# Cutting the last attention chunk into four one-tile blocks, and dropping the filler matmuls

## The chip, the cores and the metric

One core of a Trainium2 chip runs the whole program in one launch. The metric is the device time of that launch in microseconds (us). The kernel before has a median of 1463.39 us in four runs (1460.27 to 1465.49).

Engine names are those of the profile: PE is the matrix engine, PEld its weight loads, DVE the vector engine, ACT the scalar engine, POOL the GpSimd engine, SPq the queue that issues the DMAs.

A ratio in this text is the mean time of one kernel's fast runs over the mean time of the fast runs of the kernel before in the same rounds. It is therefore not quite the ratio of the medians that stand beside it.

## The reference

A layer norm feeds a 32-head attention and a SwiGLU, and both are added to the input. S = 2048, D = 512, head size 16.

```python
xn  = layernorm(A_x)                               # [1, 2048, 512]
q,k,v = split(xn @ wqkv)                           # 32 heads of 16
p   = softmax(q @ k.T * 16**-0.5)                  # 2048 x 2048 for each head
att = (p @ v) @ wo
glu = (silu(xn @ w1) * (xn @ w3)) @ w2
out = A_x + att + glu
```

## The kernel before

Attention is done in 32 blocks: 8 groups of 4 heads, times 4 chunks of 512 queries. A block goes through two stages, and the second stage of block n runs beside the first stage of block n+1.

1. Max: PE makes the scores with the queries on the partitions, DVE takes row maxima (32 reductions of 128x1024). The negated maxima go through POOL, a DVE transpose and nine DMAs, and become two extra rows of the query operand `QM`.
2. Exp: PE makes the scores again with the keys on the partitions. The extra rows of `QM` subtract the maximum. ACT takes `exp` (64 tiles of 128x512), PE multiplies by V ("PV"), ACT copies the result, three DMA steps bring the reciprocal row sums to where POOL multiplies with them.

```python
def max_block(n):
    g, cc = blocks[n]                              # 4 tiles of 128 queries in a chunk cc
    for tl_ in range(4):
        for kc in range(NCH):
            for j0 in (0, 1):
                u = max_units[mu_ctr[0] % 2]       # PSUM banks (0,1) or (2,3)
                ...                                # 2 matmuls into u, reduce_max of u     (L846, L857)
    ...                                            # negate, split in two, transpose       (L861..L873)
    S.dma(... scr_nm[par] <- NMT ...)              #                                       (L875)
    for j in range(4):
        for hl in range(2):
            S.dma(... QM[prt, r, j % 2, cc*512:(cc+1)*512] <- scr_nm ...)              # (L885)
```

Ahead of the exps stands a filler. It is a dummy matmul after every second exp from number 1900 on (there are 2048), meant to keep the clock of PE up, and it writes PSUM bank 3:

```python
FILL_BANK = 3
...
S.add("act", emit_ex, ...)                         # exp                                   (L923)
if fill_from is not None and idx >= fill_from and (idx - fill_from) % fill_every == 0:
    def emit_fill(e):
        return e.matmul(bank(FILL_BANK), IDENT, ...)                                   # (L930)
    fill_tasks.append(S.add("pe", emit_fill, ..., writes=[hz_bank[FILL_BANK]], extra=[ta], stream="fill"))
```

The output projection of a 128-row tile needs all 8 head groups. What it waits for is kept per chunk of 512 queries:

```python
S.add("pool", ... ATTNT[:, g, cc*512:(cc+1)*512] = OT * RB ..., writes=[hz_attnt[g][cc]])   # (L1002)
...
for t0 in range(0, NT, 2):
    cc = t0 // 4
    chains.append(dict(..., reads=[hz_attnt[g][cc] for g in range(G)] + [hz_wop]))          # (L684)
```

All instructions of an engine run in an order that is fixed when the program is built: a small scheduler inside the source plans it from estimated durations, and dependencies follow the order in which the source names the buffers. Whatever writes bank 3 earlier in the source must be done before a later writer of bank 3.

Of the kernel before, what the change touches and what calls it, by code (L numbers as in the profile page):

```python
# [359 lines left out]
def bass_parallel_sum__mha_block__glu_gated_swiglu__prompt_kernel(  # L360
# [15 lines left out]
    if A_x.shape[1] == 2048 and A_x.shape[2] == 512 and B_w1.shape[1] == 1792:  # L376
        cfg.setdefault("max_after", "glu2_0_0_0")
        cfg.setdefault("fill_from", 1900)
        cfg.setdefault("fill_every", 2)
    ACT_EXP_DUR = cfg.get("act_exp_dur", 500)  # L380
    FILL_BANK = 3
# [18 lines left out]
    PV_BATCH = 3  # L400
    NBLK = G * NCH
# [60 lines left out]
    with ExitStack() as stack:  # L462
# [87 lines left out]
        hz_qm = [[[_Buf("qm%d_%d_%d" % (r, v, cc)) for cc in range(NCH)] for v in range(2)] for r in range(R_QM)]  # L550
# [43 lines left out]
        S.add("pool", lambda e: e.memset(VAUG[:, :, :, 0:1], 1.0), writes=hz_vaug, dur=200 + NT * H, name="vones", stream="init")  # L594

# [151 lines left out]
        for r in range(R_QM):  # L747
            for v in range(2):
                for cc in range(NCH):
                    hz_qm[r][v][cc].inherit(*hz_xn)  # L750
# [57 lines left out]
        blocks = [(g, cc) for g in range(G) for cc in range(NCH)]  # L808
# [22 lines left out]
        def max_block(n):  # L831
            g, cc = blocks[n]
            r = g % R_QM
            par = n % 2
            for tl_ in range(4):
                qt = 4 * cc + tl_
                for kc in range(NCH):
                    for j0 in (0, 1):
# [3 lines left out]
                        def emit_mm(e, u=u, j0=j0, qt=qt, kc=kc, tl_=tl_):  # L842
                            ins = None
                            for i, j in enumerate((j0, j0 + 2)):
                                h = j // 2
                                ins = e.matmul(bank(u[i]), QM[64 * h:64 * h + 64, r, j % 2, qt * 128:(qt + 1) * 128],  # L846
                                               KAUG[64 * h:64 * h + 64, g, kc * 512:(kc + 1) * 512],
                                               start=True, stop=True, tile_position=(64 * h, 0))
                            return ins
                        S.add("pe", emit_mm, reads=[hz_qm[r][j0 % 2][cc], hz_kaug[g][kc]], writes=[hz_bank[u[0]], hz_bank[u[1]]],  # L850
                              extra=[max_gate[0]] if (n == 0 and tl_ == 0 and kc == 0 and j0 == 0) else [],
                              dur=216, name="maxS%d_%d_%d_%d" % (n, tl_, kc, j0), stream="max", mode="64x128")
                        base = tl_ * 4 * NCH + j0 * NCH + kc
                        st = 2 * NCH

                        def emit_mx(e, u=u, base=base, st=st, par=par):
                            return e.reduce_max(MPART[:, par, base:base + st + 1:st],  # L857
                                                ps[:, u[0] * 512:(u[0] + 2) * 512].rearrange("p (a b) -> p a b", a=2), axis=AX.X)
                        S.add("dve", emit_mx, reads=[hz_bank[u[0]], hz_bank[u[1]]], pwrites=[hz_mpart[par]], dur=1139,
                              name="max%d_%d_%d_%d" % (n, tl_, kc, j0), stream="max")  # L860
            S.add("dve", lambda e, par=par: e.tensor_reduce(MFIN[:, par, :], MPART[:, par, :].rearrange("p (a k) -> p a k", k=NCH),  # L861
                                                           AX.X, ALU.max),
                  reads=[hz_mpart[par]], writes=[hz_mfin[par]], dur=135, name="mfin%d" % n, stream="small")
            nmv = NM[:, par, :].rearrange("p (t l j) -> p t l j", t=4, l=2, j=4)
            S.add("pool", lambda e, par=par: e.tensor_scalar(T32[:, par, :], MFIN[:, par, :], -4.0, 0.0, op0=ALU.mult, op1=ALU.add),  # L865
                  reads=[hz_mfin[par]], writes=[hz_t32[par]], dur=250, name="t32_%d" % n, stream="negm")
            S.add("pool", lambda e, par=par, nmv=nmv: e.tensor_scalar(nmv[:, :, 0, :], T32[:, par, :].rearrange("p (t j) -> p t j", t=4),
                                                                    1.0, 0.0, op0=ALU.mult, op1=ALU.add),
                  reads=[hz_t32[par]], writes=[hz_nm[par]], dur=250, name="nmhi_%d" % n, stream="negm")
            S.add("pool", lambda e, par=par, nmv=nmv: e.tensor_tensor(nmv[:, :, 1, :], T32[:, par, :].rearrange("p (t j) -> p t j", t=4),  # L870
                                                                    nmv[:, :, 0, :], ALU.subtract),
                  reads=[hz_t32[par], hz_nm[par]], writes=[hz_nm[par]], dur=300, name="nmlo_%d" % n, stream="negm")
# [5 lines left out]
            for j in range(4):  # L878
                for hl in range(2):
                    prt = 32 * j + 16 + hl  # L880

                    def emit_sc(e, j=j, hl=hl, prt=prt, par=par):
                        dst = QM[prt:prt + 1, r, j % 2, cc * 512:(cc + 1) * 512]
                        src = scr_nm[par].rearrange("(b t k) x -> k t b x", b=4, t=4, k=8)[4 * hl + j]
                        return e.dma_start(dst, src)  # L885
                    S.dma(emit_sc, reads=[hz_scrnm[par]], pwrites=[hz_qm[r][j % 2][cc]], nbytes=1024, name="nmsc%d_%d_%d" % (n, j, hl),
                          stream="nmt", ring="nmt", group=grp)
# [14 lines left out]
        fill_tasks = []  # L902

        def emit_exp_unit(tiles):
# [5 lines left out]
            n, kt, j = tile  # L910
            g, cc = blocks[n]
            r = g % R_QM
            h = j // 2

            def emit_mm(e):
                return e.matmul(bank(b), KAUG[64 * h:64 * h + 64, g, kt * 128:(kt + 1) * 128],  # L916
                                QM[64 * h:64 * h + 64, r, j % 2, cc * 512:(cc + 1) * 512],
                                start=True, stop=True, tile_position=(64 * h, 0))
            S.add("pe", emit_mm, reads=[hz_kaug[g][kt // 4], hz_qm[r][j % 2][cc]], writes=[hz_bank[b]], dur=216,
                  name="expS_%d_%d_%d" % tile, stream="exp", mode="64x128")  # L920
# [7 lines left out]
            if fill_from is not None and idx >= fill_from and (idx - fill_from) % fill_every == 0:  # L928
                def emit_fill(e):
                    return e.matmul(bank(FILL_BANK), IDENT, KAUG[:, g, kt * 128:kt * 128 + 512] if kt * 128 + 512 <= S_ else KAUG[:, g, 0:512],  # L930
                                    start=True, stop=True)
                fill_tasks.append(S.add("pe", emit_fill, reads=[hz_const, hz_kaug[g][kt // 4]], writes=[hz_bank[FILL_BANK]], extra=[ta],
                                        dur=216, name="fill%d" % idx, stream="fill", mode="128x128"))
# [7 lines left out]
        pvstate = {}  # L941

        pv_pending = []

        def flush_pv():
# [5 lines left out]
            def emit_pv(e, sets=sets):  # L951
                ins = None
                for (n, kt, slots) in sets:
                    g, cc = blocks[n]
                    for j in range(4):
                        ins = e.matmul(ps[32 * j:32 * j + 17, PVB * 512:(PVB + 1) * 512], VAUG[:, kt, 4 * g + j, :],  # L956
                                       PT[:, slots[j], :], start=(kt == 0), stop=(kt == NKT - 1), tile_position=(0, 32 * j))
                return ins
            rd = []
            for (n, kt, slots) in sets:  # L960
                rd += [hz_pt[s_] for s_ in slots] + [hz_vaug[kt]]
            S.add("pe", emit_pv, reads=rd, writes=[hz_bank[PVB]], dur=232 * len(sets),
                  name="pv%d_%d_x%d" % (sets[0][0], sets[0][1], len(sets)), stream="pv", mode="128x32")

        def yield_pv():
            while True:
# [3 lines left out]
                keys = [(n, kt, j) for j in range(4)]  # L970
# [3 lines left out]
                pv_pending.append((n, kt, slots))  # L974
                for k in keys:
                    del tile_slot[k]
                last = (kt == NKT - 1)
                if len(pv_pending) >= PV_BATCH or last:
# [8 lines left out]
        def finish_block(n):  # L987
            g, cc = blocks[n]
            rr = n % 2
            S.add("act", lambda e, rr=rr: e.activation(OT[:, rr, :], bank(PVB), ACT.Copy), reads=[hz_bank[PVB]], writes=[hz_ot[rr]],  # L990
                  dur=690, name="pvev%d" % n, stream="pvevac")
            S.dma(lambda e, rr=rr: e.dma_start(LC[:, rr, :], OT[0:128:32, rr, :]), reads=[hz_ot[rr]], writes=[hz_lc[rr]],
                  nbytes=8192, name="lgath%d" % n, stream="norm", ring="norm")
            S.add("dve", lambda e, rr=rr: e.reciprocal(RC[:, rr, :], LC[:, rr, :]), reads=[hz_lc[rr]], writes=[hz_rc[rr]],  # L994
                  dur=250, name="recip%d" % n, stream="nrm")
            S.dma(lambda e, rr=rr: e.dma_start(scr[rr], RC[:, rr, :]), reads=[hz_rc[rr]], writes=[hz_scr[rr]],
                  nbytes=8192, name="rc2d%d" % n, stream="norm", ring="norm")
            grp = []
            for j in range(4):
                S.dma(lambda e, rr=rr, j=j: e.dma_start(RB[32 * j + 1:32 * j + 17, rr, :], scr[rr, j:j + 1, :].broadcast_to([16, 512])),  # L1000
                      reads=[hz_scr[rr]], pwrites=[hz_rb[rr]], nbytes=32768, name="rbb%d_%d" % (n, j), stream="norm", ring="norm", group=grp)
            S.add("pool", lambda e, rr=rr, g=g, cc=cc: e.tensor_tensor(ATTNT[:, g, cc * 512:(cc + 1) * 512], OT[:, rr, :], RB[:, rr, :], ALU.mult),  # L1002
                  reads=[hz_ot[rr], hz_rb[rr]], writes=[hz_attnt[g][cc]], dur=1270, name="attn%d" % n, stream="attn")

        LAG = 1
        for n in range(NBLK + LAG):
            if n < NBLK:
                g, cc = blocks[n]
                if cc == 0 and g + 1 < G:
                    pass  # L1010
                if cc == 0 and g >= 1:
# [3 lines left out]
            if m >= 0:  # L1015
                for kt in range(NKT):
                    for j in range(4):
                        pend.append((m, kt, j))
                    form_units()
        form_units(flush=True)  # L1020
        yield_pv()
# [89 lines left out]
```

## Time and profile before

| what | value | view |
|---|---|---|
| time | 1463.39 us (4 runs) | times |
| DVE busy from 300 to 1300 us | 98.8% | windows |
| block 30: exps on ACT | 1356.89 to 1390.77 us | timeline of ACT |
| block 31 (the last): max ends | 1390.91 us | timeline of DVE |
| ACT idle before block 31's exps | 8.61 us, and 0.71 us before the copy | timeline of ACT |
| last exp to the end of the span | 20.7 us | timeline, page |

These two lines are from the page of the kernel before: the engines' shares of the chain that ended last, and the costliest group (line, engine, operation, shapes, count, busy us, mean ns, idle before).

```profile
DVE 66%; PE 25%; ACT 4%; SPq 2%; DMA 2%; issue 1%; POOL 0%; POOLq 0%
L857 DVE TENSOR_REDUCE arena<-ps 128x2 f32<-128x1024 f32 x1024 | 1170.6, 1211 | 172.8 <-PE ps L846 167.8
```

The row maxima on DVE carry two thirds of the chain that ended last. They bound the long middle of the kernel, which the change leaves alone. The change is about what comes after them. The next lines are the timeline of ACT at the end: start, duration, line, operation, count, and in brackets the idle time before and what ended it.

```profile
1390.17 0.60 ACT L923 ACTIVATE arena<-ps 128x512 bf16<-128x512 f32 x1 [0.37 <-PE ps L916]
1391.48 0.60 ACT L990 ACTIVATE arena<-ps 128x512 f32<-128x512 f32 x1 [0.71 <-PE ps L956]
1400.68 1.57 ACT L923 ACTIVATE arena<-ps 128x512 bf16<-128x512 f32 x3 [8.61 <-PE ps L916]
...
1405.28 3.08 ACT L923 ACTIVATE arena<-ps 128x512 bf16<-128x512 f32 x6 [0.50 <-PE ps L916]
...
1435.36 2.07 ACT L923 ACTIVATE arena<-ps 128x512 bf16<-128x512 f32 x4 [0.27 <-PE ps L916]
1437.96 0.60 ACT L990 ACTIVATE arena<-ps 128x512 f32<-128x512 f32 x1 [0.53 <-PE ps L956]
```

ACT finishes block 30, copies, and then waits 8.61 us, because the maxima of block 31 end only at 1390.9 and their DMAs have to follow. From 1405.28 to 1437.43 it does 58 exps, 0.554 us each. Last, the timeline of PE from the last PV on, and two windows of the same stretch (after the interval and its length: PE, PEld, DVE, ACT and POOL busy, granted PE clock, DMA share, GB/s).

```profile
1437.84 9.67 PE L930 MATMUL ps<-arena 128*128 128x512 bf16 x43
1447.35 7.07 PE L684 MATMUL ps<-arena 128*128 128x512 bf16 x32
1454.26 3.62 PE L930 MATMUL ps<-arena 128*128 128x512 bf16 x16
1440.00:1444.00 4.00, 4.00 (x20) 1.86 (x19) 0.25 (x1) 0.00 (x0) 0.00 (x0) 1.00 0.11 19
1444.00:1448.00 4.00, 3.95 (x20) 1.76 (x18) 0.00 (x0) 0.00 (x0) 1.26 (x1) 1.00 0.05 16
```

During the normalisation by DMA (1438.6 to 1445.5) PE runs fillers (L930), the clock stays at 1.00, and the projection of the last four tiles (32 matmuls) takes 7.07 us.

### The profile page before, as it was taken

How to read it: one execution, taken by the hardware profiler on the slowest of the kernel's cores; microseconds unless marked ns; L12 is line 12 of the kernel's file. 1: busy time of each engine (PE TensorE's matmuls, PEld its weight loads, DVE VectorE, ACT ScalarE, POOL GpSimd, SP SyncE). 2: the span in 40 equal slices, each digit the busy share in tenths (PEclk: the TensorE clock that was granted, in tenths of full speed). 3: DMA queues.
4: the chain of work that ended last, by engine and by line, in shares of the span. 5: the costliest groups of instructions: out<-in, count | busy, mean ns of one | idle time of the engine just before them, and what ended most of it. 6: DMA issues, size and time to landing. Idle time of an engine off the chain costs nothing.

```text
span 1458.1 us, 20711 instructions
## 1 busy us (share of the span) xinstructions
PE 1294.4 (89%) x8144; PEld 391.1 (27%) x8170; DVE 1217.4 (83%) x1215; ACT 1182.5 (81%) x2299; POOL 182.2 (12%) x225
## 2 busy tenths in 40 slices
PE   3999999989888899888888888888998888888889
PEld 2334432322222222222222222222222222222223
DVE  7000089999999999999999999999999999998831
ACT  1775542379999999999899999999999998888764
POOL 0205543320010001000100010001000000000000
PEclk9999999999999999999999999999999999998999
DMA  6000000010000000000000000000000000000011
GB/s 252 2 2 0 1 1 1 1 16 5 6 5 6 6 5 8 6 6 5 6 5 6 5 6 5 5 6 5 6 5 6 5 6 5 6 5 5 5 34 34
DMA packets 31138, 18.39 MB, mean 13 GB/s; under 512 B 21056, under 2 KB 27456, under 8 KB 31040
## 3 DMA queue, kind: packets, MB, share of 16 engines
q1 hardware_dynamic: 31040, 17.06, 4.4%
q8 instruction: 64, 1.05, 0.3%
q14 instruction: 34, 0.28, 0.1%
HBM read 14.16 MB, written 2.62 MB: 12 GB/s over the span
## 4 chain that ended last, share of the span: by engine, by line
DVE 66%; PE 25%; ACT 4%; SPq 2%; DMA 2%; issue 1%; POOL 0%; POOLq 0%
DVE arena L857 64%; PE ps L684 13%; PE ps L704 4%; ACT arena L923 4%; PE ps L846 3%; PE ps L916 3%; SPq L885 2%; PE ps L956 1%; PE ps L930 1%; DMA arena<-scr_nm 1%; DVE arena L613 1%; DMA scr_nm<-arena 1%; DVE arena L629 0%; DVE arena L994 0%; DMA arena<-arena 0%
## 5 line engine op out<-in xcount | busy, mean ns | idle before, releaser
L857 DVE TENSOR_REDUCE arena<-ps 128x2 f32<-128x1024 f32 x1024 | 1170.6, 1211 | 172.8 <-PE ps L846 167.8
L923 ACT ACTIVATE arena<-ps 128x512 bf16<-128x512 f32 x2048 | 1029.3, 644 | 98.1 <-PE ps L916 93.3
L916 PE MATMUL ps<-arena 64*128 64x512 bf16 x2048 | 688.9, 391 | 71.7 <-DMA arena<-scr_nm 16.4
L846 PE MATMUL ps<-arena 64*128 64x512 bf16 x2048 | 438.7, 393 | 59.1 <-DVE arena L857 44.3
L916 PEld LDWEIGHTS ps<-arena 64*128 64x128 bf16 x2048 | 181.1, 94 | 490.7 <-ACT arena L923 440.6
L684 PE MATMUL ps<-arena 128*128 128x512 bf16 x841 | 202.7, 382 | 6.2 <-POOL arena L785 3.8
L846 PEld LDWEIGHTS ps<-arena 64*128 64x128 bf16 x2048 | 99.8, 93 | 318.0 <-DVE arena L857 266.9
L956 PE MATMUL ps<-arena 128*17 128x512 bf16 x2048 | 146.6, 385 | 1.0 <-ACT arena L923 0.9
L1002 POOL TENSOR_TENSOR arena<-arena 128x512 bf16<-128x512 f32 x32 | 40.5, 1266 | 623.7 <-DMA arena<-scr_rinv 623.7
L684 PEld LDWEIGHTS ps<-arena 128*128 128x128 bf16 x864 | 74.9, 98 | 109.5 <-issue 25.4
L785 POOL TENSOR_TENSOR arena<-arena 128x512 bf16<-128x512 bf16 x56 | 64.5, 1152 | 89.5 <-ACT arena L783 89.5
L704 PE MATMUL ps<-arena 128*16 128x512 bf16 x1024 | 61.4, 386 | 1.2 <-DVE arena L649 0.9
L956 PEld LDWEIGHTS ps<-arena 128*17 128x17 bf16 x2048 | 36.9, 89 | 72.3 <-issue 50.9
L801 ACT ACTIVATE arena<-ps 128x512 f32<-128x512 f32 x16 | 9.8, 610 | 56.1 <-PE ps L684 56.1
L783 ACT ACTIVATE arena<-ps 128x512 bf16<-128x512 f32 x56 | 33.4, 597 | 26.6 <-PE ps L684 26.6
L781 ACT ACTIVATE arena<-ps 128x512 bf16<-128x512 f32 x56 | 33.4, 597 | 25.5 <-PE ps L684 25.5
L865 POOL TENSOR_SCALAR arena<-arena 128x16 f32<-128x16 f32 x32 | 6.6, 206 | 373.4 <-DVE arena L861 373.0
L1047 DVE TENSOR_TENSOR arena<-ps,arena 128x512 bf16<-128x512 f32 x16 | 11.1, 691 | 46.7 <-PE ps L684 46.7
L739 POOL TENSOR_SCALAR arena<-arena 128x2048 bf16<-128x2048 bf16 x16 | 31.4, 1977 | 125.3 <-PE ps L916 65.2
L704 PEld LDWEIGHTS ps<-arena 128*16 128x16 bf16 x1024 | 20.4, 89 | 41.9 <-ACT arena L712 13.5
L712 ACT ACTIVATE arena<-ps,arena 128x512 bf16<-128x512 f32 x32 | 24.9, 778 | 8.1 <-PE ps L704 6.7
L643 PE MATMUL ps<-arena 128*128 128x128 bf16 x64 | 7.5, 312 | 24.2 <-DVE arena L629 24.2
(45 smaller groups left out, 178.9 us busy)
## 6 DMA issues: line engine op xcount, KB each, us to landing
arena<-in_B_w_dram SPq DMA_DIRECT2D x3, 1792.0 KB, 19.0
arena<-scr_nm SPq DMA_DIRECT2D x256, 1.0 KB
arena<-scr_rinv SPq DMA_DIRECT2D x128, 32.0 KB, 1.8
arena<-in_A_x_dram SPq DMA_DIRECT2D x4, 512.0 KB, 6.1
out_dram<-arena SPq DMA_DIRECT2D x16, 128.0 KB, 1.7
arena<-in_A_wqkv_dram SPq DMA_DIRECT2D x1, 1536.0 KB, 11.8
scr_nm<-arena SPq DMA_DIRECT2D x32, 8.0 KB, 1.4
arena<-in_A_wo_dram SPq DMA_DIRECT2D x4, 128.0 KB, 4.3
```

The source lines that it names most:

```text
L684: ins = e.matmul(ps[:, ch["bank"] * 512:ch["bank"] * 512 + ch["n"]], ch["lhs"](kk), ch["rhs"](kk), start=(kk == 0), stop=(kk == nk - 1))
L704: ins = e.matmul(ps[32 * j:32 * j + DH, b * 512:(b + 1) * 512], WQKV[:, dc, hcol:hcol + DH], XNT[:, dc, tc * 512:(tc + 1) * 512], start=(d ...
L739: S.add("pool", lambda e, r=r, v=v, msk=msk: e.tensor_scalar(QM[:, r, v, :], QUN[:, g, :], msk, 0.0, op0=ALU.mult, op1=ALU.add), reads=hz_ ...
L781: S.add("act", lambda e, bg=bg, rg=rg: e.activation(SG[:, rg, :], bank(bg), ACT.Silu), reads=[hz_bank[bg]], writes=[hz_sg[rg]], dur=600, n ...
L783: S.add("act", lambda e, bu=bu, rg=rg: e.activation(UB[:, rg, :], bank(bu), ACT.Copy), reads=[hz_bank[bu]], writes=[hz_ub[rg]], dur=690, n ...
L785: S.add("pool", lambda e, rg=rg, fc=fc: e.tensor_tensor(HT[:, fc, :], SG[:, rg, :], UB[:, rg, :], ALU.mult), reads=[hz_sg[rg], hz_ub[rg]], ...
L846: ins = e.matmul(bank(u[i]), QM[64 * h:64 * h + 64, r, j % 2, qt * 128:(qt + 1) * 128], KAUG[64 * h:64 * h + 64, g, kc * 512:(kc + 1) * 51 ...
L857: return e.reduce_max(MPART[:, par, base:base + st + 1:st], ps[:, u[0] * 512:(u[0] + 2) * 512].rearrange("p (a b) -> p a b", a=2), axis=AX.X)
L916: return e.matmul(bank(b), KAUG[64 * h:64 * h + 64, g, kt * 128:(kt + 1) * 128], QM[64 * h:64 * h + 64, r, j % 2, cc * 512:(cc + 1) * 512] ...
L923: return e.activation(PT[:, slot, :], bank(b), ACT.Exp, scale=0.25)
L956: ins = e.matmul(ps[32 * j:32 * j + 17, PVB * 512:(PVB + 1) * 512], VAUG[:, kt, 4 * g + j, :], PT[:, slots[j], :], start=(kt == 0), stop=( ...
L1002: S.add("pool", lambda e, rr=rr, g=g, cc=cc: e.tensor_tensor(ATTNT[:, g, cc * 512:(cc + 1) * 512], OT[:, rr, :], RB[:, rr, :], ALU.mult), ...
```

## The change

The intent: the last chunk is cut into four blocks of one tile (128 queries). The first of them can go through max, negation and DMA while ACT still does block 30, and what follows the last exp gets narrower. So that an exp tile stays 128x512, a small block puts four key tiles side by side into one bank, with four 128-column matmuls. The fillers are switched off by default; where they are asked for, they are placed behind the last max. The core of the diff:

```diff
-        cfg.setdefault("fill_from", 1900)
-        cfg.setdefault("fill_every", 2)
...
-        blocks = [(g, cc) for g in range(G) for cc in range(NCH)]
+        thin_chunks = cfg.get("thin_chunks", 1)
+        blocks = []
+        for g in range(G):
+            for cc in range(NCH):
+                if g * NCH + cc >= G * NCH - thin_chunks:
+                    for tl_ in range(4):
+                        blocks.append((g, cc, 4 * cc + tl_, 1))
+                else:
+                    blocks.append((g, cc, 4 * cc, 4))
...
-                return e.matmul(bank(b), KAUG[64*h:64*h+64, g, kt*128:(kt+1)*128],
-                                QM[64*h:64*h+64, r, j % 2, cc*512:(cc+1)*512], ...)
+                for i, kt in enumerate(kts):        # 1 key tile, or 4 in a small block
+                    ins = e.matmul(ps[:, b*512 + i*qw:b*512 + (i+1)*qw],
+                                   KAUG[64*h:64*h+64, g, kt*128:(kt+1)*128],
+                                   QM[64*h:64*h+64, r, j % 2, qt0*128:qt0*128 + qw], ...)
...
+                    ins = e.matmul(ps[32*j:32*j+17, PVB*512:PVB*512 + qw], VAUG[:, kt, 4*g + j, :],
+                                   PT[:, slots[j], sub*qw:(sub+1)*qw], ...)                # PV
...
-            S.add("pool", ... ATTNT[:, g, cc*512:(cc+1)*512] ..., writes=[hz_attnt[g][cc]])
+            S.add("pool", ... ATTNT[:, g, c0:c0 + qw] ..., pwrites=[hz_attnt[g][cc]])
```

The hazards of `QM` are kept per tile of 128 queries. The output projection still waits for `hz_attnt[g][cc]`, the whole chunk.

## The prediction

> **What bounds the kernel now.** Up to 1391 us it is VectorE: the chain of waits gives 63.7% of the span to the row-max reductions (1024, mean 1211 ns); DVE is over 98% busy from 300 to 1300 us (table of windows). None of that changes. The change can touch only the last 115 us. There, in the timeline:
> - the last block's max runs 1351.7 to 1390.9 and starts 4 us late: filler matmuls write PSUM bank 3, which the max units use;
> - ACT idles from 1390.8 to 1400.7 (apart from a 0.6 copy) while max, negate, transpose and nine DMA issues pass before the last scores;
> - the last 64 exps take 1400.7 to 1437.4, 0.57 us each against 0.51 unhindered, because PE mixes in the output projection;
> - PV, copy, normalisation by three dependent DMA steps (1438.6 to 1445.5), multiply 1.27, projection of four tiles 1447.35 to 1454.4, store: 20.7 us from last exp to end.
>
> **What the change does.**
> 1. Four one-tile blocks: the first three get their max while ACT still does block 30. The ACT gap goes: 9 to 10 us.
> 2. Fillers gone: the last max ends near 1388, so the fourth tile is ready before its turn.
> 3. PE pays. A score unit of one 512-column matmul becomes four of 128 columns with four weight loads; PV becomes 16 narrow matmuls per four units. The trace shows 216 ns for 512 columns and 58 ns per load-and-matmul pair in the column-tiled QK projection; it has no warm 128-column stream. The Trainium skill (TensorE: Matmul & The Clock Gate, Back-to-back issue gap) gives about 81 ns per matmul sustained at 128 columns; no run here shows it yet. I estimate, per four units, 1.0 to 1.3 us scores, 0.3 to 0.9 PV, 0.2 mode changes: 1.5 to 2.4 us against ACT's 2.05. With the 96 projection matmuls (20.7 us plus switches), a third of which now runs free in the ACT gap, the last exps become PE-bound: 43 to 53 us from 1390.5, ending near 1438 (1433 to 1444). The gap's gain is nearly spent here.
> 4. After the last exp: narrower copy (-0.3), multiply (-0.85), DMAs (-0.2). But the fillers kept PE warm from 1437.8 to 1447.4. Without them PE idles some 8 us; after a like gap at 1311.7 to 1316.3 the granted clock was 0.50 for about 5 us. The last projection (7.07 us) should take about 9: +2. It still waits for all four small blocks.
>
> **Sum.** -10 (gap), +6 to +16 (PE; 2 for extra copies and PV-bank handovers inside it) less what ends early, -1.3 and +2 at the end. I expect about -4: **1459 us**, range 1446 to 1474. Chances: faster by over 2% 0.03, within 2% 0.94, slower by over 2% 0.03. An ideal split could win about 15 us (1%).
>
> **What the profile would show.** Right: no ACT gap over 2 us between 1380 and 1400; PE over 90% busy and ACT under 85% from 1391 to the last exp, exps 0.65 to 0.8 us apart; last max before 1389; in the last projection a granted clock of 0.5 to 0.7 and spacing up to 430 ns at its start. Stages before 1340 us the same within 1 us.
>
> **What would make it wrong.** Weight loads fully hidden and PV four-fold parallel (55 ns a round): exps run at ACT's pace, end near 1428, time 1447. Or weight loads exposed, some 110 ns per pair: 1472. PE's static order may place projections so that they delay scores, or leave some for the idle end, which would keep PE warm.

## The result, and the profile after

The changed kernel takes 1455.14 us (median of 10 runs, 1453.83 to 1458.21); the kernel before took 1464.85 us in 16 runs. The ratio is 0.9941, with a 95% interval of 0.9930 to 0.9952: about 8.6 us less, within 2%.

The same views of the changed kernel. First the page: the reductions, now L867, cost what they did.

```profile
DVE 66%; PE 25%; ACT 4%; DMA 2%; SPq 2%; issue 1%; POOL 0%; POOLq 0%
L867 DVE TENSOR_REDUCE arena<-ps 128x2 f32<-128x1024 f32 x1024 | 1171.1, 1209 | 173.1 <-PE ps L856 168.1
```

Then the timeline of ACT (L945 are the exps, L1017 the copies):

```profile
1390.39 4.70 ACT L945 ACTIVATE arena<-ps 128x512 bf16<-128x512 f32 x9 [0.30 <-PE ps L936]
1395.25 1.08 ACT L945 ACTIVATE arena<-ps 128x512 bf16<-128x512 f32 x2 [0.16 <-PE ps L936]
1396.22 0.60 ACT L1017 ACTIVATE arena<-ps 128x512 f32<-128x512 f32 x1
1396.70 3.06 ACT L945 ACTIVATE arena<-ps 128x512 bf16<-128x512 f32 x6
1400.08 2.07 ACT L945 ACTIVATE arena<-ps 128x512 bf16<-128x512 f32 x4 [0.31 <-PE ps L936]
...
1431.02 1.09 ACT L945 ACTIVATE arena<-ps 128x512 bf16<-128x512 f32 x2 [0.31 <-PE ps L936]
1432.89 0.28 ACT L1017 ACTIVATE arena<-ps 128x128 f32<-128x128 f32 x1 [0.78 <-PE ps L973]
```

The 8.61 us are gone. Block 30's last exp is the seventh of the nine in the first line (about 1394.1), and the first exp of the first small block follows it at once. From 1396.70 to 1432.11 there are 60 exps, 0.590 us each, with the 0.28 us copies of three small blocks among them. And the timeline and windows of PE (L936 scores, L973 PV, L685 projection):

```profile
1408.20 1.04 PE L685 MATMUL ps<-arena 128*128 128x512 bf16 x4
1409.17 0.64 PE L936 MATMUL ps<-arena 64*128 64x128 bf16 x12
1409.73 0.40 PE L973 MATMUL ps<-arena 128*17 128x128 bf16 x16
1410.25 0.39 PE L936 MATMUL ps<-arena 64*128 64x128 bf16 x4
...
1432.77 4.49 PE L685 MATMUL ps<-arena 128*128 128x512 bf16 x19
1441.14 9.81 PE L685 MATMUL ps<-arena 128*128 128x512 bf16 x32 [3.88 <-POOL arena L1029]
1440.00:1444.00 4.00, 2.86 (x7) 1.03 (x8) 0.00 (x0) 0.00 (x0) 0.45 (x1) 0.50 0.10 34
1444.00:1448.00 4.00, 4.00 (x14) 1.54 (x13) 1.16 (x2) 0.00 (x0) 0.00 (x0) 0.66 0.10 33
```

PE goes idle for 3.88 us before the last projection, finds its clock at 0.50, and needs 9.81 us for the 32 matmuls that took 7.07.

Absolute times of two profiles can't be compared directly: the closing reduction of block 30's max, which both kernels reach with the same PE instructions almost up to there, fell between 1346.65 and 1350.78 us in the twelve profiles that share them. So the table counts from that reduction (t0). The column "control" is a second profile of the kernel before (the run `base` below). Each entry is the time in the timeline less t0.

| event, us after t0 | before | control | after |
|---|---|---|---|
| t0 itself | 1346.65 | 1350.38 | 1348.96 |
| last max closed | 44.3 | 44.4 | 41.0 |
| block 30's last exp ends | 44.1 | 44.3 | 45.1 |
| first of the last 64 exps starts | 54.0 | 54.4 | 45.1 |
| last exp ends | 90.8 | 91.1 | 83.2 |
| last projection starts | 100.7 | 101.0 | 92.2 |
| last projection ends | 107.8 | 108.1 | 102.0 |
| span ends | 111.5 | 111.8 | 104.9 |

The change wins 9 us at the start of the last exps, gives back 1.4 while they run, wins 1 in the copy, DMAs and multiply, gives back 2.7 in the cold projection, and wins 0.7 after it. From t0 on that is 6.5 to 6.9 us; the timed difference is 7.0 to 10.3 us by its interval. So the profiles come out just below the interval; the rest can't be told from their scatter before t0. Which part of the 9 us is the split's and which the fillers' is for the run `nofill` below.

### The profile page after: what moved, and what is told of

Its sections match the earlier page's. It is cut to its first block, busy times and chain, and to the rows that moved or that the text cites. A ratio compares the mean times of both kernels' runs of the same rounds, so it can differ in the third digit from the quotient of the medians.

```text
span 1453.9 us, 21408 instructions
## 1 busy us (share of the span) xinstructions
PE 1284.7 (88%) x8451; PEld 394.4 (27%) x8480; DVE 1218.6 (84%) x1224; ACT 1182.8 (81%) x2302; POOL 184.6 (13%) x238
## 4 chain that ended last, share of the span: by engine, by line
DVE 66%; PE 25%; ACT 4%; DMA 2%; SPq 2%; issue 1%; POOL 0%; POOLq 0%
DVE arena L867 64%; PE ps L685 13%; PE ps L705 4%; PE ps L856 3%; ACT arena L945 3%; PE ps L936 3%; SPq L896 1%; PE ps L973 1%; DVE arena L614 1%; DMA arena<-scr_nm 1%; DMA scr_nm<-arena 1%; DVE arena L630 0%; DMA arena<-arena 0%; DVE arena L1021 0%; DMA arena<-scr_rinv 0%
## 5 line engine op out<-in xcount | busy, mean ns | idle before, releaser
L867 DVE TENSOR_REDUCE arena<-ps 128x2 f32<-128x1024 f32 x1024 | 1171.1, 1209 | 173.1 <-PE ps L856 168.1
L945 ACT ACTIVATE arena<-ps 128x512 bf16<-128x512 f32 x2048 | 1030.0, 644 | 92.6 <-PE ps L936 87.2
L936 PE MATMUL ps<-arena 64*128 64x512 bf16 (+1 forms) x2240 | 689.2, 371 | 68.0 <-DMA arena<-scr_nm 12.8
L856 PE MATMUL ps<-arena 64*128 64x512 bf16 x2048 | 439.7, 393 | 60.5 <-DVE arena L867 46.2
L936 PEld LDWEIGHTS ps<-arena 64*128 64x128 bf16 x2240 | 188.2, 94 | 485.4 <-ACT arena L945 438.2
L685 PE MATMUL ps<-arena 128*128 128x512 bf16 x835 | 203.5, 384 | 10.9 <-POOL arena L1029 3.9
L856 PEld LDWEIGHTS ps<-arena 64*128 64x128 bf16 x2048 | 99.7, 93 | 319.3 <-DVE arena L867 268.4
L973 PE MATMUL ps<-arena 128*17 128x512 bf16 (+1 forms) x2240 | 150.9, 371 | 1.5 <-ACT arena L945 1.4
L1029 POOL TENSOR_TENSOR arena<-arena 128x512 bf16<-128x512 f32 (+1 forms) x35 | 41.1, 1173 | 611.4 <-DMA arena<-scr_rinv 611.4
L685 PEld LDWEIGHTS ps<-arena 128*128 128x128 bf16 x864 | 75.2, 98 | 111.8 <-issue 23.4
L973 PEld LDWEIGHTS ps<-arena 128*17 128x17 bf16 x2240 | 39.4, 89 | 72.5 <-issue 50.3
L876 POOL TENSOR_SCALAR arena<-arena 128x16 f32<-128x16 f32 (+1 forms) x35 | 7.2, 204 | 376.7 <-DVE arena L872 376.3
```

The lines of the kernel that those rows point to most:

```text
L685: ins = e.matmul(ps[:, ch["bank"] * 512:ch["bank"] * 512 + ch["n"]], ch["lhs"](kk), ch["rhs"](kk), start=(kk == 0), stop=(kk == nk - 1))
L856: ins = e.matmul(bank(u[i]), QM[64 * h:64 * h + 64, r, j % 2, qt * 128:(qt + 1) * 128], KAUG[64 * h:64 * h + 64, g, kc * 512:(kc + 1) * 51 ...
L867: return e.reduce_max(MPART[:, par, base:base + st + 1:st], ps[:, u[0] * 512:(u[0] + 2) * 512].rearrange("p (a b) -> p a b", a=2), axis=AX.X)
L936: ins = e.matmul(ps[:, b * 512 + i * qw:b * 512 + (i + 1) * qw], KAUG[64 * h:64 * h + 64, g, kt * 128:(kt + 1) * 128], QM[64 * h:64 * h + ...
L945: return e.activation(PT[:, slot, :], bank(b), ACT.Exp, scale=0.25)
L973: ins = e.matmul(ps[32 * j:32 * j + 17, PVB * 512:PVB * 512 + qw], VAUG[:, kt, 4 * g + j, :], PT[:, slots[j], sub * qw:(sub + 1) * qw], st ...
```

## The experiments

Theory A: the gain is the split, because the first pieces' max and DMA chain pass under block 30's exps. The fillers had to go for that, since their bank holds back the max. Their absence costs clock at the end. Rival B: the gain is that of dropping the fillers (whose bank delayed the last max), and PE pays the split back. Then there was the question of what the change leaves unused, and of what paces the last exps. All runs are of one core; each kernel was correct. `oldfill`, `base`, `projlate` and `projlate_dummy` were run once, so their state is unknown, and they are used for their profiles.

### Without the split: `nofill`

```diff
-        thin_chunks = cfg.get("thin_chunks", 1)
+        thin_chunks = cfg.get("thin_chunks", 0)
```

> The new source with the split turned off: only the fillers are gone. Theory A (split does the work): the last max no longer waits for the fillers and ends about 4 us earlier after its predecessor (36 to 40 us, not 44.3), so the ACT gap shrinks from 9.9 to about 6 us, but the last projection starts cold and takes 9.8 us, not 7.1: net -1 us, ratio to before 0.998 to 1.001. Rival B (the gain of the change is that of dropping the fillers, and the split is paid back by PE): ratio about 0.994, as with the split.

Measured: 1462.04 us, ratio 0.9986 (0.9972 to 0.9999). Lines of DVE (closing reduction), ACT and PE:

```profile
1390.89 0.22 DVE L872 TENSOR_REDUCE arena<-arena 128x16 f32<-128x64 f32 x1
1400.74 1.58 ACT L945 ACTIVATE arena<-ps 128x512 bf16<-128x512 f32 x3 [3.34 <-PE ps L936]
1447.83 9.13 PE L685 MATMUL ps<-arena 128*128 128x512 bf16 x31 [7.10 <-POOL arena L1029]
```

Its t0 is 1349.94, so the last max closes 41.0 us after it: 3.3 to 3.5 us earlier than with fillers. The first of the last 64 exps starts 50.8 us after t0, not 54.0 or 54.4, so 3.2 to 3.6 of the 9 us that the change wins at this point come from dropping the fillers, and 5.7 from the split. PE then idles 7.10 us, and the last projection takes 9.13 us, where the expectation had 9.8. In all, dropping the fillers alone wins about 2 us (1 was expected), inside the range of theory A. Rival B falls.

### The split with the fillers where they were: `oldfill`

```diff
-                fill_req.append((idx, ta, g))
+                fill_tasks.append(S.add("pe", emit_fill, ..., writes=[hz_bank[FILL_BANK]], extra=[ta], ...))
```

(and fillers on from exp 1900.)

> The split with the fillers where they were in the old source: inside the exp units, writing bank 3 before the next max block may. Theory A (the fillers' bank holds back the max): max of the second small block cannot start before the fillers tied to the exps of block 30 are done, so three small max blocks (27 us of DVE) come after about 1390 us; an ACT gap over 10 us per small block, total 10 to 25 us above before. Rival (fillers only cost PE time): 1 to 3 us above the changed kernel, no new ACT gap.

Measured: 1481.7 us in one run, 17 us above the median of before (1464.5). The timeline of DVE:

```profile
1366.47 0.21 DVE L884 STREAM_TRANSPOSE arena<-arena 128x32 bf16<-128x32 bf16 x1 [0.88 <-POOL arena L881]
1394.11 0.25 DVE L1024 RECIPROCAL arena<-arena 128x16 f32<-128x16 f32 x1 [27.43 <-DMA arena<-arena]
1395.30 8.02 DVE L867 TENSOR_REDUCE arena<-ps 128x2 f32<-128x1024 f32 x7 [0.94 <-PE ps L856]
```

After the first small block's max, DVE, the engine that bounds the kernel, stands idle for 27 us. The max of the second small block needs bank 3, the fillers tied to block 30's exps come before it in the source and write bank 3, so it waits for all those exps. ACT later waits 13.96, 4.62 and 7.86 us for the small blocks (over 10 us for each was expected, which only the first reached). So the fillers had to be dropped or moved for the split to work.

### The changed kernel with a warm end: `endwarm`

```diff
+        for i_ in range(16):                       # after the last PV
+            S.add("pe", <dummy matmul into bank 3>, extra=[last_pv[0], last_max[0]], stream="fill")
```

> The changed kernel plus 16 dummy matmuls after the last PV, in the PE's idle time before the last projection. Theory A (cold clock): the granted clock stays near 1 through the last projection, which takes 7.1 us and not 9.8; total -2.5 us against the changed kernel, ratio to before about 0.9924. Rival: the projection is slow for another reason (reads, writes to the bank still drained): 9.8 us as before, ratio 0.994.

Measured: 1453.55 us, ratio 0.9926 (0.9912 to 0.9940). PE:

```profile
1437.97 3.62 PE L1058 MATMUL ps<-arena 128*128 128x512 bf16 x16
1442.30 7.08 PE L685 MATMUL ps<-arena 128*128 128x512 bf16 x31 [0.71 <-POOL arena L1030]
```

The granted clock is 1.00 through the whole end, and the projection takes 7.08 us. So the projection was slow because of the clock.

### No split, warm end: `nofill_warm`

The two edits above together, with 36 dummy matmuls.

> No split, no fillers, but 36 dummy matmuls after the last PV that keep the PE clock up. With the run without split and fillers (0.9986) this gives what dropping the fillers would have won had the end stayed warm: theory A 2 to 2.5 us below that run, ratio 0.9965 to 0.9975, last projection 7.1 us. Rival (clock not the cause): 0.9986 again. The split's own part is then the distance from this run to the changed kernel with a warm end (0.9926): 6 us.

Measured: 1460.97 us, ratio 0.9972 (0.9958 to 0.9986); the last projection takes 7.07 us, and the span ends 2.95 us after it, against 3.7 in the kernel before, which still ran 16 fillers there. The four ratios make a small table:

| | cold end | warm end |
|---|---|---|
| no split, no fillers | 0.9986 | 0.9972 |
| split | 0.9941 | 0.9926 |

Down a column the split is worth 0.0045 and 0.0046 of the time before, 6.6 us. Along a row a cold end costs 0.0014 and 0.0015, 2.1 us. The intervals are each about 0.0013 either way, but both differences come out alike twice.

### Two halves in place of four quarters: `half`

```diff
-                    for tl_ in range(4):
-                        blocks.append((g, cc, 4 * cc + tl_, 1))
+                    for tl_ in (0, 2):
+                        blocks.append((g, cc, 4 * cc + tl_, 2))
```

(and two key tiles of 256 columns to a bank.)

> The changed kernel with the last chunk cut into two halves of 256 queries and not four of 128. Theory A (what pays is that the first piece's max and its DMA chain pass under block 30's exps; how narrow a piece is hardly matters): no ACT gap either, after the last exp 0.5 us more for wider copy and multiply, ratio to before 0.993 to 0.996. Rival (the narrow last piece is what pays, by the shorter end): 3 us or more slower than with four, ratio over 0.996.

Measured: 1455.4 us, ratio 0.9943 (0.9931 to 0.9956), the same as with four. ACT never waits over 1 us between block 30's and the last exps. How narrow a piece is hardly matters here; that there is a first piece to go ahead does. A part of the sameness is luck, though: in the profile the last projection starts 0.9 us later after t0 than with four pieces (93.1 and 92.2 us), but takes 8.55 us, not 9.81, because the clock was back at 1.00 3.0 us after its start, not 5.6 us.

### The projection's dependency per tile: `pertile`

```diff
-        hz_attnt = [[_Buf(...) for cc in range(NCH)] for g in range(G)]
+        hz_attnt = [[_Buf(...) for qt in range(NT)] for g in range(G)]
-            ... pwrites=[hz_attnt[g][cc]]
+            ... writes=[hz_attnt[g][qt0 + i_] for i_ in range(nq)]
-                                   reads=[hz_attnt[g][cc] for g in range(G)] + [hz_wop]))
+                                   reads=[hz_attnt[g][t] for g in range(G)] + [hz_wop]))
```

> The changed kernel with the dependency of the output projection on the normalised attention kept per 128-query tile instead of per 512-query chunk. Theory A (the change left its best part unused, since the last four tiles still wait for the last small block): tiles 12 to 14 are projected in the idle time of PE, 8 matmuls and not 32 stand after the last multiply, and they run warm: 6 to 8 us less than the changed kernel, ratio to before 0.988 to 0.990. Rival (PE has a backlog of projections then anyway): at most 3 us less, ratio 0.992 or more.

Measured: 1450.03 us, ratio 0.9899 (0.9883 to 0.9916), 6 us below the changed kernel. PE after the last PV:

```profile
1434.21 11.40 PE L685 MATMUL ps<-arena 128*128 128x512 bf16 x51
```

Tiles 12 to 14 are projected while the last small block is being normalised. PE no longer idles, so no dummy is needed to keep the clock at 1.00, and the last eight matmuls follow at once. The change had cut the attention into tiles but left the consumer waiting for the chunk.

### A control: `base`

The kernel before, unchanged.

> The kernel before, unchanged, profiled once more as a control. If the profile of before is typical, every boundary up to 1347 us lies within 3 us of it and the stages after it have the same lengths within 0.5 us (last max 44 us after the one before, last 64 exps 36.8 us, last projection 7.1 us); the 2.3 us by which the changed kernel's profile reached that boundary later is then scatter, since both run the same instructions up to there.

Measured: 1464.31 us in one run; t0 came at 1350.38, 3.7 us later than in the first profile of the same kernel, so the 3 us of the expectation were too few; the stages after t0 agree within 0.4 us (table above). The first profile was of that kernel's fastest run.

### What paces the last exps: `projlate`, `projlate_dummy`, `pertile_pv8`

`projlate` makes every projection wait for the last PV.

```diff
+                                   extra=[last_pv[0]],
                                    reads=[hz_attnt[g][cc] for g in range(G)] + [hz_wop]))
```

> The changed kernel with every output projection held back behind the last PV: a measurement, meant to be slower. Theory A (projections on PE set the pace of the last 64 exps): the exps of a small block take 8.3 to 8.6 us (ACT's own pace, 16 x 0.51 and the copy), not 9.5; total 4 to 12 us above the changed kernel since 128 projection matmuls then stand in a row. Rival (the narrow matmuls and mode changes set the pace): 9.3 us or more per small block.

Measured: 1467.96 us in one run. A small block took 9.6 us (its copies start at 1405.20, 1414.81 and 1424.41), as slow as with the projections in between. That doesn't decide between the two, for something else changed. One window:

```profile
1405.00:1410.00 5.00, 4.43 (x74) 2.83 (x68) 0.18 (x1) 4.50 (x10) 0.00 (x0) 0.50 0.04 4
```

Without the projections the PE clock fell to 0.50 at 1389.8 us and was back at 1437.6, 4.2 us after the projections had begun. The run had changed two things at once. `projlate_dummy` was to mend that, with a dummy of 512 columns ahead of every other score unit, in the mode of the scores (64 of the 128 rows).

```diff
+                if nq != 4 and idx % 2 == 0:
+                    e.matmul(bank(b), KAUG[64*h:64*h+64, g, 0:128], KAUG[64*h:64*h+64, g, 0:512], ...)
```

> Projections held back behind the last PV as in the run before that showed a clock of 0.50, but with one dummy 512-column matmul, in the mode of the scores, ahead of every other small score unit, to keep the clock up; slower in total on purpose. Theory C (in that run it was the halved clock of PE, not the narrow matmuls as such, that kept a small block at 9.6 us; in the changed kernel it is the projections' share of PE): granted clock 1.00 from 1395 us to the last exp, and a small block takes 8.3 to 8.8 us. Rival D (one PV flush per four exps costs ACT a stall of 0.3 us, whatever else PE does): 9.4 us or more, one ACT stall of 0.3 us per four exps still there.

Measured: 1473.88 us in one run, and the clock still at 0.50, though PE was now busy without a break:

```profile
1415.00:1420.00 5.00, 5.00 (x67) 3.67 (x66) 0.00 (x0) 3.99 (x9) 0.46 (x1) 0.50 0.01 3
```

So neither run could separate its theories. What `projlate` does show, since its edit moves nothing but the projections, is that in the changed kernel it is the projections (128 rows, 512 columns) between the narrow matmuls that keep the clock at 1.00. Which property of them matters isn't shown: from 800 to 1300 us of the kernel before, PE ran only scores of 64 rows and PVs of 17 columns, with 512 moving columns each, at a mean clock of 0.98. `pertile_pv8` halves the number of PV groups in the small blocks, on top of `pertile`.

```diff
-                if (len(pv_pending) >= (PV_BATCH if nq == 4 else 4) and unit_done) or last:
+                if (len(pv_pending) >= (PV_BATCH if nq == 4 else 8) and unit_done) or last:
```

> The per-tile projection dependency, and PV of the small blocks flushed every eight score units and not every four (half the mode changes for PV). Rival D of the run beside it (PV flushes set the pace): a small block takes 8.9 to 9.1 us and not 9.5, last exp 1.5 to 2.5 us earlier. Theory C (PE's total work sets the pace): 9.3 us or more. In both the end is the PE's backlog of projections, so the total gains at most 2 us on the per-tile run: ratio to before 0.9885 to 0.990.

Measured: 1448.94 us, ratio 0.9900 (0.9883 to 0.9917), the same as `pertile`. From the first full group on, 60 exps took 34.45 us (1396.64 to 1431.09), 0.574 each, against 35.41 (0.590) in `pertile`. That is 1 us earlier, less than the 1.5 to 2.5 of rival D, and no gain in the total. The time of a small block doesn't help: the copies are 9.56 and 8.23 us apart (mean 8.9, which would be rival D's figure), but with 17 and 14 exps between them. How the remaining 0.590 divides between PV groups, projections and narrow scores stays open.

### Dummies at the block boundaries: `pertile_gap`

At the start of a late block PE waits for the maxima, and the clock is low there as well: in the changed kernel it was at 0.50 from 1354.5 to 1368.2 us. PE's longest wait in it, 3.01 us, ended at 1358.6; the clock had fallen before that wait began. This run puts 14 dummies there at blocks 28, 29 and 30, on top of `pertile`.

```diff
+                if 28 <= m <= 30:
+                    for i_ in range(14):
+                        S.add("pe", <dummy matmul into the bank of block m's first scores>, stream="fill", mode="64x128")
```

> The per-tile projection dependency, and 14 dummy matmuls in PE's wait for the maxima at the starts of blocks 28, 29 and 30, in the mode of the scores. Theory (PE cools there: the clock was 0.50 from about 1355 to 1368 us, and ACT stalled 1.35 us behind a PV at half clock): clock 1.00 through that stretch, the stall gone, 1 to 1.5 us gained per boundary on the way to the last max or the last exp: ratio to before 0.986 to 0.989. Rival (the wait for the DMA hides it, or the dummies delay the max matmuls): no gain, 0.9895 or more.

Measured: 1447.45 us, ratio 0.9886 (0.9870 to 0.9903). It has the lowest median of all, but its interval overlaps that of `pertile`, so it isn't shown to be better. In the profile the clock stayed at 1.00 up to 1358.9 us and was then at 0.50 only twice for 3.4 us. t0 came at 1343.23 us, 7 us earlier than in `pertile`, and most of that was lost again in block 30. One reason stands in POOL's timeline:

```profile
1364.68 1.26 POOL L1029 TENSOR_TENSOR arena<-arena 128x512 bf16<-128x512 f32 x1 [11.14 <-DMA arena<-scr_rinv]
1366.03 0.19 POOL L876 TENSOR_SCALAR arena<-arena 128x4 f32<-128x4 f32 x1
```

The second small block's maxima were closed at 1361.90 us. Their negation (L876) stands in POOL's fixed order behind the multiply of block 29 (L1029), which waited for its DMAs; DVE then waited 3.62 us for POOL and ACT 2.32 us. In the changed kernel POOL has the same order, but there the second block's maxima closed only at 1372.58 us, when the multiply (1365.09 to 1366.36) was long done. That this is the whole of what was lost was not tried.

## Why the prediction was right

It forecast 1459 us (1446 to 1474) and a time within 2%; measured were 1455.14 us. The gain was forecast as about 4 us against 1463.39, and measured as about 8.6 us. The direction and the parts were right. One term, the price on PE, was mis-sized: the sum had +6 to +16 us for it, and measured were 1.4. The forecast within 2% risked little, as even an ideal split was put at 15 us (1%); the test of the mechanism is in the parts.

- "The ACT gap goes: 9 to 10 us": right. First of the last 64 exps at 45.1 us after t0, not 54.0 or 54.4.
- "The last max ends near 1388": right on the profile's own clock. It closed 41.0 us after t0, which is 1387.7 us with the t0 of before; on the clock of the changed kernel's profile it was 1390.0, and the mark "before 1389" missed.
- "PE pays ... 1.5 to 2.4 us" for four score units, and "43 to 53 us" for the last exps: this is the step that was mis-sized. The fence above shows it. From the start of 12 score matmuls to the start of PV 0.56 us pass, from PV to the next scores 0.52 with the wait for ACT (0.42 in the cycle before), and four scores occupy 0.33 before the next projection starts: 1.3 to 1.4 us. The last exps took about 38 us (1394.1 to 1432.1), 1.4 more than before. I had taken 81 ns for a 128-column matmul from the Trainium skill (TensorE: Matmul & The Clock Gate, Back-to-back issue gap). The trace has 8 of them in 0.62 us and 4 in 0.39 us (1397.20 and 1400.73), so 57 ns from one to the next; the same section's figure for matmuls without weight loads between them, 56 ns, is the one that fits, since each load (94 ns) ran beside the matmul before it. And 16 PV matmuls lie within 0.40 us: they start in groups of four, the four column tiles within 10 ns of each other. These are the conditions that I had named for exps at ACT's pace, an end near 1428 us and a time of 1447. They held, and the exps still took 0.590 us each and not 0.51, so that conditional was wrong; what holds them is the open question of `pertile_pv8`. Of ACT I had said "under 85%" busy; it was 89% from 1395 to 1430 us (31.27 of 35.00), with PE at 93%; and the exps, forecast at 0.65 to 0.8 us, came 0.590 apart.
- "PE's static order may ... leave some for the idle end": it did. Nineteen projection matmuls ran after the last PV (1432.77 to 1437.3), which also took load off the exps; I had put it among the things that would make me wrong.
- "narrower copy (-0.3), multiply (-0.85), DMAs (-0.2)": the stretch from last exp to last projection is 9.0 us, not 9.9, so -0.9 and not -1.35. The multiply and copy are as said (0.45 and 0.28 us), but the DMAs gained nothing: from the issue of the first to the issue of the last kind it took 4.4 us (1433.19 to 1437.58) against 3.6 (1438.59 to 1442.14), with stores of earlier tiles issued in between. Whether the stores cause it was not tried. That such a chain is longer than its slices is what the Trainium skill says (Perfetto Trace Analysis, DMA Instruction — HWDGE): the slice shows the issue and not the movement of data. The trace agrees: the first DMA's slice is 0.58 us, and the reciprocal that waits for it starts 1.87 us after the start of that slice (1438.59 to 1440.46).
- "Without them PE idles some 8 us ... The last projection should take about 9: +2": right in kind, and 9.81, so +2.7. The idle time was 3.88 us, shorter than forecast, and still long enough. The Trainium skill (TensorE: Matmul & The Clock Gate, Part 1) says that an idle window of about 3.4 us halves the clock; the trace has 0.50 after the 3.88 us, and `endwarm` 1.00 after 0.71, but the clock fell at 1439.9 us already, 2.6 us after the last matmul ended (by its modelled end).
- The end of the fillers themselves had been overlooked: 16 of them ran to 1457.9 us of a span of 1458.1, and without them the span ends 0.7 us sooner after the last projection.
- "It still waits for all four small blocks": right, and worth 6 us, as `pertile` shows. I had noted it without costing what it leaves unused.
- "Stages before 1340 us the same within 1 us": missed. t0 differs by 2.3 us between the two profiles, and by 3.7 us between two profiles of the kernel before, so this mark tested only the scatter.

## What to carry to other kernels

A stage that hands over to the next through a chain of small steps should have its last piece cut so that the chain of the first part passes under other work; one cut was enough here. Then follow the smaller pieces to every consumer and keep its dependency at the same grain, or the end of the pipeline waits as before. Dummy matmuls that keep the clock up belong into the idle time alone, and into a bank that nobody on the critical path needs.

## What the Trainium skill lacked or had wrong

- TensorE: Matmul & The Clock Gate, Back-to-back issue gap: it gives about 81 ns for a sustained 128-column matmul with its weight load. In the changed kernel such pairs, with 64 rows, followed each other at 57 ns (8 in 0.62 us, 4 in 0.39 us), in short runs.
- TensorE: Matmul & The Clock Gate, Part 1: it ties the full clock to some 3.4 us of PE activity. In `projlate_dummy` PE was busy 5.00 of 5.00 us in window after window with matmuls of 64 rows and of 17 columns, and the granted clock stayed at 0.50 from 1391.4 to 1442.6 us, 51 us; the 128-row matmuls of 512 columns had begun at 1440.6. The spacing agrees with the clock: four score matmuls lie within 0.63 us there, and within 0.39 us in the changed kernel. PE's busy time is modelled, so how full the array was isn't shown. Part 1 doesn't say how far matmuls that fill a part of the array count as activity.
- The same part: recovery took longer than one window after block boundaries. In the changed kernel PE worked again from 1358.6 us, and the clock was back only at 1368.2; from 1361.4 to 1364.8 PE was busy for all of 3.40 us at 0.50. Nor did the fall need an idle window: it came at 1354.5, and from 1351.1 to 1354.5 PE had been busy for 2.08 of 3.40 us.
- No page says what dummy matmuls ahead of a last stage bring in a whole kernel: here 0.0014 to 0.0015 of the time, 2.1 us, from 36 of them without the split and 16 with it.
